# Holding the first weight transfers of a fused RWKV-7 and GELU kernel behind the decays of chunk 1

## The chip, the cores and the metric

The kernel runs on one core of a Trainium2 chip. The metric is device time in microseconds, the median of several executions; one more execution is taken with the hardware profiler, and all views come from it. The engines are named TensorE (PE; PEld is its weight load), VectorE (DVE), ScalarE (ACT), GpSimd (POOL) and SyncE (SP, which only issues transfers). Each runs its own instructions in the order in which the kernel writes them. Transfers are issued from SyncE's queue or from GpSimd's, and run on the core's 16 DMA engines.

## The reference

An attention block with a recurrent state (RWKV-7), then a feed-forward block with an exact GELU:

```python
batch, n_heads, seq, head_dim = (4, 8, 768, 40)      # r, k, v, w, a, b; w between 0.85 and 0.95
n_tokens, d_model, d_ff = (3072, 320, 2048)          # x, w_in, w_out
...
    for t in range(S):
        ...
        y[:, :, t] = np.einsum('bhd,bhde->bhe', rt, state)
        Sa = np.einsum('bhde,bhe->bhd', state, at)
        state_decay = state * wt[:, :, None, :] - np.einsum('bhd,bhe->bhde', Sa, bt)
        state = state_decay + np.einsum('bhd,bhe->bhde', vt, kt)
...
    h = x @ w_in                                     # x: y as (B*S, H*D)
    g = 0.5 * h * (1.0 + erf(h * inv_sqrt2))
    return (g @ w_out).astype(np.float32)
```

The two weight matrices come as 64-bit floats, and the kernel turns them into 32-bit floats itself.

## The kernel before

The sequence is cut into 12 chunks of 64 steps. Within a chunk the recurrence is written as products of small matrices and the inverse of a triangular one; between chunks only the state is carried. All four batches and eight heads of a chunk are worked on together. A chunk's outputs go through the feed-forward block (`ph`, `gelu`, `po` and later a form with seven products) while later chunks are worked on. The order of all work on all five engines is written out by hand, step by step; each engine runs its share in that order.

The steps of the first chunks that matter here:

- `load_w`, `fetch`, `load_a` (line 194 issues the transfers) bring w, b and a of chunks 0 and 1, in this order, from SyncE. The a rows of chunk 1 land in the tile `spare_raw`. Behind them SyncE issues v (`load_VR(0)`), r (`load_r(0)`), k (`fetch(0, 'k')`) and the second part of the first matrix (`first_load(False, 1)`).
- `logs`, `sums_cum` and `exp_cum` give a chunk's decays: a logarithm on ScalarE, sums over the steps as products on TensorE, an exponential on ScalarE (line 526).
- `flip_b`, `copy_b` (the transposes `nT_ps`, line 571, and the copy at line 645) and `turn_a`, `scale_a` (the transposes `aT_ps`, line 571, and the product at line 625) lay out b and a of a chunk.
- `mask_Z`, `turn_Z`, `start_T`, `square`, `turn_square`, `copy_square` and `add_square` invert chunk 0's triangular matrix by repeated squaring. `start_T` is four additions on GpSimd (line 903).
- `first_load(last, part, at, eng)` brings one part of the first matrix, as raw words, in six transfers (lines 431, 433, 434). Part 0 lands in the tile of the second matrix (`w_out_sb`), in columns that are free until that matrix comes; it is issued from GpSimd's queue.
- `U[n]` is the conversion of one tile of raw words, in the steps a, r, m, b, s and g on VectorE, ScalarE and, for some tiles, GpSimd. `U[0].a` (line 371) is the first to read the raw words, parts 0 and 1 of them.

Tiles that take turns in memory have a common tag and a count of buffers (`bufs=2`); a new tile takes the place of the one before last with that tag, and its first writer waits for the last reader of that one. Waits between engines are derived from what each instruction reads and writes: an instruction that writes where another has written waits for it.

The place of the edit in the written order:

```python
    scale_a(0)
    first_load(False, 0, early(0, 4), eng=nc.gpsimd)
    copy_b(0)
    make_N(0)
    mask_N(0)
    exp_cum(1)
    scale_b(1)
```

On GpSimd's own queue the next instructions behind this `first_load` are those of `start_T(0, nc.gpsimd)`, then `scale_k(0)` (line 610) and the elimination steps `substitute(1, ...)` (lines 833 and 835).

Of the kernel before, what the change touches and what calls it, by code (L numbers as in the profile page):

```python
# [21 lines left out]
def kernel(  # L22
# [46 lines left out]
    nc = tc.nc  # L69
# [209 lines left out]
    early_w = SM.rearrange("p e g n c -> p (e g n c)")[:, :G * H * HP]  # L279
    early_k = work.tile([P, G, NP, P], FP32, tag="rT", name="early_k", bufs=2).rearrange("p g n t -> p (g n t)")  # L280
    ahead = {n: t[:, :G * DM].rearrange("p (g h d) -> p g h d", g=G, h=H) for n, t in (("b", early_b), ("k", early_k))}
# [78 lines left out]
    class Unit:  # L360
# [4 lines left out]
        def a(self):  # L365
            w = self.words()
            n = w.shape[1] // 2
            self.lo, self.hi = (w.rearrange("p (n x) -> p n x", x=2)[:, :, x] for x in range(2))
            both = work.tile([P, LW], UINT32, tag="conv", name="conv", bufs=2)
            self.power, self.mant = both[:, :n], both[:, LW // 2:LW // 2 + n]  # L370
            nc.vector.tensor_scalar(self.power, self.hi, 0x7FF00000, None, ALU.bitwise_and)  # L371
# [30 lines left out]
    def first_load(last, part, at=None, eng=nc.sync):  # L402
# [16 lines left out]
        for x in range(2):  # L419
# [6 lines left out]
            else:  # L426
# [5 lines left out]
                if x:  # L432
                    eng.dma_start(out=words[half(x, D), n], in_=src[x, x, part, :, n])
                    eng.dma_start(out=words[x * HP + D:, n], in_=src[1 - x, x, part, :REST, 0])

    def second_load(f, slot, at=late_raw, eng=nc.sync):

        src = moe_w_out.bitcast(UINT32) if wide_out else moe_w_out
        to = w_out_sb[:, f]
        if wide_out:  # L440
            to = second_raw[f] = at[:, slot * DM:(slot + 2) * DM]
        to, rows = (t.rearrange("p (n m) -> p n m", m=P if wide_out else HP) for t in (to, src[f * P:(f + 1) * P]))
        for n in range(2):
            eng.dma_start(out=to[:, n::2], in_=rows[:, n::2])
# [107 lines left out]
    def turn_part(c, blocks):  # L552
        t = turned_in[c]
        if "part" not in t:
            t["part"] = by_batch(side("part", "conv", 2))
# [60 lines left out]
    def scale_a(c):  # L616
        t = turned_in[c]
        wp = t["wp"].rearrange("p (e n) t -> p e n t" if c > NB else "p (n e) t -> p e n t", e=2)[:, :, :, :C]
        if c < NT:
            aT = work.tile([P, 2, G, NP, C], FP32, tag="aT", name="aT", bufs=2)  # L620
# [33 lines left out]
    def turn_k(c):  # L654
        t = turned_in[c]
        if c >= NB:
            kT = t["k_turned"] = by_batch(side("k_turned", "conv", 2))
            turn(kT, c, "k_turned")
            return
        flip_k(c)  # L660
        copy_k(c)
# [40 lines left out]
    def turn_r(c):  # L702
        if c < NT:
            flip_r(c)
            copy_r(c)
            return
        rT = side("rT", "rT", 2)
        turn(rT.rearrange("p q m (e t) -> p (q m e) t", e=2), c, "r")
        turned_in[c]["rT"] = parts(rT)
# [5 lines left out]
    def copy_r(c):  # L715
        rT = side("rT", "rT", 2)
        nc.scalar.copy(rT, turned_in[c].pop("rT_ps"))
        turned_in[c]["rT"] = parts(rT)
# [135 lines left out]
    def turn_inverse(c):  # L854
        W = inverses[c]
        if c < NB:
            to = turned_in[c].pop("Nb") if c > 1 else work.tile([P, BL * BL], FP32, tag="Nb", name="Nb")
            L, T = to[:, :NBL * BL], to[:, NBL * BL:]
        else:
            L = work.tile([P, NBL * BL], FP32, tag="conv", name="L", bufs=2)  # L860
            T = W.rearrange("p s t -> p (s t)")
# [344 lines left out]

    def half_tile(tag, bufs):
        return work.tile([P, NF // 2, P], FP32, tag=tag, name="half", bufs=bufs)

    def seven(c):  # L1210
        t1, t2, t4 = sums_of_w
        t3 = quarter(0, 1)
        os = [work.tile([P, 2, DM // 2], FP32, tag="os", name="os", bufs=2) for g in range(G)]
        c11, c12, c21, c22 = os[0][:, 0], os[0][:, 1], os[1][:, 0], os[1][:, 1]
# [25 lines left out]
        m1, m2 = yield from products_of(0, (block(0, 0), quarter(0, 0)), (block(0, 1), quarter(1, 0)), apart=True)  # L1240
        s1 = half_tile("conv", 2)
        nc.vector.tensor_tensor(s1, block(1, 0), block(1, 1), ALU.add)
        while between:
            new_state(between.pop(), range(1, G))
        if c >= NCH - 2:
            s2 = half_tile("conv", 2)
        else:
# [28 lines left out]
    class Seven:  # L1276

        def __init__(self, c):
            self.c = c
            self.os = [work.tile([P, 2, DM // 2], FP32, tag="os", name="os", bufs=2) for g in range(G)]  # L1280
            self.c11, self.c12, self.c21, self.c22 = (self.os[n // 2][:, n % 2] for n in range(4))
# [14 lines left out]
        def s1(self):  # L1296
            self.one = half_tile("conv", 2)
            nc.vector.tensor_tensor(self.one, block(1, 0), block(1, 1), ALU.add)  # L1298

        def s2(self):  # L1300
            if self.c >= NCH - 2:
                self.two = half_tile("conv", 2)
            else:
# [94 lines left out]
    def put(c, g):  # L1398
        os = work.tile([P, DM], FP32, tag="os", name="os", bufs=2)
        nc.vector.tensor_copy(os, pos[c][:, g])  # L1400
# [178 lines left out]
    copy_r(1)  # L1579
    spare_rT = words("rT", 2)  # L1580
    first_load(True, 1, spare_raw[:, :LW], eng=nc.sync)
# [706 lines left out]
```

## Time and profile before

| | |
|---|---|
| median of 3 runs | 648.96 us (647.38 to 650.41) |
| the profiled execution | 651.05 us, span 649.3 us |
| TensorE busy | 628.7 us, 97% |
| VectorE, ScalarE, GpSimd busy | 452.6, 375.3, 387.0 us |
| mean granted TensorE clock | 0.993 |
| moved by SyncE's queue, by GpSimd's queue | 56.46 MB, 1.70 MB |

The span runs from the first to the last instruction of the profiled execution; its own time holds what lies around the span too. A row of the timeline gives start and length in us, engine, line of the kernel, operation, the tile written and the tiles read, partitions x elements, the count of instructions put together, and in brackets how long the engine had been idle and what ended that. A row of the stretches gives the stretch, its length, the busy time of PE, PEld, DVE, ACT and POOL (with instructions), the granted TensorE clock, the share of the DMA engines and GB/s. A row of a DMA queue gives packets, MB and the time of the packets as a share of 16 engines; the software queue is GpSimd's, the hardware queue SyncE's. The chain of waits is followed back from the last instruction: at each step to what released it.

### The profile page before, as it was taken

What the parts mean: (1) busy time and instruction counts of PE and PEld (TensorE: products, weight loads), DVE (VectorE), ACT (ScalarE), POOL (GpSimd) and SP (SyncE); (2) the same over time, 40 slices, a digit from 0 to 9 for tenths busy, and PEclk for the clock granted to TensorE, in tenths of its full rate; (3) what the DMA queues carried; (4) which work ended last, traced back from release to release, by engine and by line L of the source; (5) the groups of instructions that cost most, each with busy time, mean ns of one, the idle gap of its engine ahead of it and who ended that gap; (6) DMA issues with size and microseconds to landing.
All of it is one profiled execution on the core that took longest, in us unless ns stands there. A gap on an engine that the chain in (4) does not pass through costs nothing.

```text
span 649.3 us, 32674 instructions
## 1 busy us (share of the span) xinstructions
PE 628.7 (97%) x14652; PEld 557.2 (86%) x14652; DVE 452.6 (70%) x604; ACT 375.3 (58%) x716; POOL 387.0 (60%) x806
## 2 busy tenths in 40 slices
PE   7898999999999999999899999999999999999997
PEld 5787888887878899898898998999989989989877
DVE  1684899986568788585895995995987965623312
ACT  5455875554438474746478487587587586373010
POOL 8488488804828828828717858868858768620000
PEclk9998999999999999999899999999999999999999
DMA  9995658447666125447454455464365350210100
GB/s 137 154 158 119 128 129 174 107 96 129 127 107 121 31 51 110 98 94 129 84 109 100 79 113 103 98 123 98 75 128 96 79 100 5 42 24 12 33 2 21
DMA packets 227054, 60.46 MB, mean 93 GB/s; under 512 B 208539, under 2 KB 225211, under 8 KB 226914
## 3 DMA queue, kind: packets, MB, share of 16 engines
q1 hardware_dynamic: 226042, 56.46, 46.5%
q0 software_dynamic: 592, 1.70, 1.3%
q8 instruction: 115, 1.88, 1.3%
q10 hardware_dynamic: 280, 0.21, 0.1%
q14 instruction: 25, 0.20, 0.1%
HBM read 50.46 MB, written 3.93 MB: 84 GB/s over the span
## 4 chain that ended last, share of the span: by engine, by line
PE 66%; POOL 15%; DVE 7%; issue 4%; ACT 3%; SPq 2%; DMA 2%; POOLq 0%; DVEq 0%; ACTq 0%
PE ph L1385 23%; PE po L1288 17%; POOL W L835 7%; POOL tmp L833 6%; PE QY L139 6%; PE po L1395 3%; PE po L1222 2%; PE J L139 2%; SPq L194 2%; DMA spare_raw<-in_a_dram 2%; PE A_ps L139 1%; PE M_ps L139 1%; PE saT_ps L139 1%; PE av L139 1%; PE RV_ps L139 1%
## 5 line engine op out<-in xcount | busy, mean ns | idle before, releaser
L1385 PE MATMUL ph<-xt,w_in_sb 64*64 64x256 f32 (+1 forms) x3360 | 218.3, 377 | 0.4 <-ACT gt L1389 0.2
L1385 PEld LDWEIGHTS ph<-xt,w_in_sb 64*64 64x64 f32 (+1 forms) x3360 | 173.4, 141 | 30.3 <-issue 1.2
L833 POOL TENSOR_TENSOR tmp<-W,Nb 128x126 f32<-128x126 f32 (+22 forms) x310 | 132.5, 427 | 64.3 <-DVE Nb L848 40.9
L835 POOL TENSOR_TENSOR W<-W,tmp 128x126 f32<-128x126 f32 (+22 forms) x310 | 139.6, 450 | 24.3
L1389 ACT ACTIVATE gt<-ph 128x1024 f32<-128x1024 f32 x48 | 49.2, 1026 | 80.1 <-PE ph L1385 76.6
L1288 PE MATMUL po<-w_out_sb,gt 128*128 128x160 f32 x576 | 84.4, 303 | 0.2 <-DVE gt L1323 0.2
L1288 PEld LDWEIGHTS po<-w_out_sb,gt 128*128 128x128 f32 x576 | 79.4, 190 | 1.8 <-issue 0.3
L1190 ACT COPY turned<-within 8x64 f32<-8x64 f32 (+3 forms) x144 | 46.4, 322 | 10.6 <-DVE within L1179 8.6
L786 POOL TENSOR_TENSOR VR<-VR,upper 128x1024 f32<-128x1024 f32 x8 | 19.3, 2414 | 35.0 <-ACT VR L782 32.8
L564 ACT COPY part<-part 32x256 f32<-32x256 f32 (+1 forms) x112 | 36.1, 322 | 1.7
L1395 PE MATMUL po<-w_out_sb,gt 128*128 128x320 f32 x128 | 36.3, 438 | 0.0
L1064 DVE STREAM_TRANSPOSE sa<-saT 128x1024 f32<-128x1024 f32 x9 | 11.2, 1242 | 35.5 <-ACT saT L1051 35.5
L1073 ACT COPY SM<-sa 32x64 f32<-32x64 f32 (+1 forms) x108 | 31.8, 294 | 2.6 <-DVE sa L1064 1.3
L1395 PEld LDWEIGHTS po<-w_out_sb,gt 128*128 128x128 f32 x128 | 23.7, 190 | 9.8 <-issue 0.5
L1311 DVE TENSOR_TENSOR os<-os,po 128x160 f32<-128x160 f32 x63 | 19.6, 314 | 18.0 <-PE po L1288 10.1
L1308 ACT COPY os<-po 128x160 f32<-128x160 f32 x9 | 2.6, 292 | 46.6 <-PE po L1288 46.5
L374 ACT ACTIVATE conv<-conv,rebias 128x320 uint32<-128x320 uint32 (+1 forms) x26 | 15.8, 621 | 20.1 <-DVE conv L371 19.9
L727 DVE TENSOR_TENSOR A<-A_ps,upper 128x1024 f32<-128x1024 f32 x12 | 14.6, 1219 | 14.0 <-PE A_ps L139 14.0
L1288 PE MATMUL po<-extra,half 128*128 128x160 f32 x160 | 23.3, 299 | 0.5 <-DVE half L1298 0.5
L727 DVE TENSOR_TENSOR SM<-M_ps,upper 128x1024 f32<-128x1024 f32 x12 | 14.7, 1223 | 11.9 <-PE M_ps L139 11.7
L1288 PEld LDWEIGHTS po<-extra,half 128*128 128x128 f32 x160 | 22.2, 190 | 0.7 <-issue 0.7
L848 DVE STREAM_TRANSPOSE Nb<-N 128x1024 f32<-128x1024 f32 x10 | 21.6, 2160 | 0.4 <-ACT N L770 0.4
(302 smaller groups left out, 1287.9 us busy)
## 6 DMA issues: line engine op xcount, KB each, us to landing
VR<-in_v_dram SPq DMA_DIRECT2D x24, 160.0 KB
out_dram<-os SPq DMA_DIRECT2D x46, 80.0 KB
b_rows<-in_b_dram SPq DMA_DIRECT2D x22, 160.0 KB
k_rows<-in_k_dram SPq DMA_DIRECT2D x22, 160.0 KB
a_pairs<-in_a_dram SPq DMA_DIRECT2D x18, 144.0 KB
r_pairs<-in_r_dram SPq DMA_DIRECT2D x36, 72.0 KB
v_pairs<-in_v_dram SPq DMA_DIRECT2D x36, 72.0 KB
a_pairs<-in_b_dram SPq DMA_DIRECT2D x16, 144.0 KB
```

Source lines behind the costliest of these rows:

```text
L139: nc.tensor.matmul(o, lhsT, rhs, start=first, stop=True, skip_group_check=True)
L564: nc.scalar.copy(to[at:at + BL, :, x, z * BL:end], tmp[on:on + BL, e, :, q * BL:q * BL + end - z * BL])
L727: nc.vector.tensor_tensor(to, pt, upper.unsqueeze(1).to_broadcast([P, 2 * G * NP, C]), ALU.mult)
L833: eng.tensor_tensor(t, W[:, :rows, j:j + 1].to_broadcast([P, rows, rest]), Nb[:, j:j + 1, j + 1:].to_broadcast([P, rows, rest]), ALU.mult)
L835: eng.tensor_tensor(W[:, :rows, j + 1:], W[:, :rows, j + 1:], t, ALU.add)
L848: nc.vector.transpose(Nb.rearrange("p s t -> p t s"), N[:, :, :BL].rearrange("p n t -> p t n").unsqueeze(2).to_broadcast([P, BL, 2, NBL]))
L1073: copy(SM[to:to + BL, g].rearrange("p q m c -> p (q m) c")[:, :, d * BL:end], t["sa"][at:at + BL, :, to:to + end - d * BL])
L1190: nc.scalar.copy(tn[to:to + deep, :, at:at + wide], within[0][at:at + deep, :, to:to + wide])
L1288: nc.tensor.matmul(self.pt[at][:, n, :DM // 2], l_[:, f], r_[:, f], start=f == 0, stop=f == NF // 2 - 1)
L1385: nc.tensor.matmul(pt[to:end, x, s], w_in_sb[half(x), kt, p * P + to:p * P + end], xt[half(x), kt], start=kt == 0, stop=kt == NK - 1)
L1389: nc.scalar.activation(gt[:, 4 * q:4 * q + 4].rearrange("p (x s) t -> p x s t", x=2), phs.pop((c, q)), ACT.Gelu)
L1395: nc.tensor.matmul(pos[c][:, g], gt[:, f, g * P:(g + 1) * P], w_out_sb[:, f], start=f == 0, stop=f == NF - 1)
```

## The change

A new step `hold(c, at)` copies eight numbers of chunk c's decays, on ScalarE, into the place where a part of the weights is going to land: two columns, 256 apart, in each of the four tiles of words. `first_load(False, 0, ...)` moves behind `hold(1, ...)` in the written order, so that its transfers, which write the same columns, wait for that copy, which waits for the exponential in `exp_cum(1)`. They are still issued from GpSimd's queue. Besides, tiles that shared places in turn by `bufs=2` get a tag for each place (`conv0` and `conv1`, `aT0` and `aT1`, `rT0` and `rT1`, `os0` and `os1`), chosen by the chunk's or the unit's number.

```diff
-    early_k = work.tile([P, G, NP, P], FP32, tag="rT", name="early_k", bufs=2).rearrange("p g n t -> p (g n t)")
+    early_k = work.tile([P, G, NP, P], FP32, tag="rT1", name="early_k").rearrange("p g n t -> p (g n t)")
...
-            both = work.tile([P, LW], UINT32, tag="conv", name="conv", bufs=2)
+            both = work.tile([P, LW], UINT32, tag=f"conv{self.n % 2 if self.n < 16 or self.n > 20 else (self.n + 1) % 2}", name="conv")
...
+    def hold(c, at):
+
+        to = at.rearrange("p (k n) -> p k n", k=NP)[:, :, :LW // 2:2 * P].bitcast(FP32)
+        given = decays[c][0][:, 0, 0, :2 * NP]
+        nc.scalar.copy(to, given.rearrange("p (k n) -> p k n", k=NP))
+
...
+    for n, unit in enumerate(U):
+        unit.n = n
...
-        aT = turned_in[c]["aT"] = work.tile([P, 2, G, NP, C], FP32, tag="aT", name="aT", bufs=2)
+        aT = turned_in[c]["aT"] = work.tile([P, 2, G, NP, C], FP32, tag=f"aT{c % 2}", name="aT")
...
     scale_a(0)
-    first_load(False, 0, early(0, 4), eng=nc.gpsimd)
     copy_b(0)
     make_N(0)
     mask_N(0)
     exp_cum(1)
+    hold(1, early(0, 4))
+    first_load(False, 0, early(0, 4), eng=nc.gpsimd)
     scale_b(1)
     sums_wT(1)
```

More of the change, by code (lines that the diff above doesn't have):

```diff
@@ L554, in turn_part @@
         if "part" not in t:
-            t["part"] = by_batch(side("part", "conv", 2))
+            t["part"] = by_batch(side("part", f"conv{c % 2}", 1))
             nc.vector.transpose(t["part"].rearrange("p n t -> p (n t)"), t["en"].rearrange("p n t -> p (n t)"))
@@ L619, in scale_a @@
         if c < NT:
-            aT = work.tile([P, 2, G, NP, C], FP32, tag="aT", name="aT", bufs=2)
+            aT = work.tile([P, 2, G, NP, C], FP32, tag=f"aT{c % 2}", name="aT")
             given = t.pop("a_ps").rearrange("p g n (e t) -> p e (g n) t", e=2)
@@ L656, in turn_k @@
         if c >= NB:
-            kT = t["k_turned"] = by_batch(side("k_turned", "conv", 2))
+            kT = t["k_turned"] = by_batch(side("k_turned", f"conv{(c + (c > 4)) % 2}", 1))
             turn(kT, c, "k_turned")
@@ L706, in turn_r @@
             return
-        rT = side("rT", "rT", 2)
+        rT = side("rT", f"rT{(c if c < 2 else c + 1) % 2}", 1)
         turn(rT.rearrange("p q m (e t) -> p (q m e) t", e=2), c, "r")
@@ L715, in copy_r @@
     def copy_r(c):
-        rT = side("rT", "rT", 2)
+        rT = side("rT", f"rT{(c if c < 2 else c + 1) % 2}", 1)
         nc.scalar.copy(rT, turned_in[c].pop("rT_ps"))
@@ L859, in turn_inverse @@
         else:
-            L = work.tile([P, NBL * BL], FP32, tag="conv", name="L", bufs=2)
+            L = work.tile([P, NBL * BL], FP32, tag=f"conv{(c + (c > 4)) % 2}", name="L")
             T = W.rearrange("p s t -> p (s t)")
@@ L1205, in weight_sums, with half_tile @@
         nc.vector.tensor_tensor(to, one_, other, ALU.subtract)
-    def half_tile(tag, bufs):
-        return work.tile([P, NF // 2, P], FP32, tag=tag, name="half", bufs=bufs)
+    def half_tile(n):
+        return work.tile([P, NF // 2, P], FP32, tag=f"conv{n % 2}", name="half")
     def seven(c):
@@ L1212, in seven @@
         t3 = quarter(0, 1)
-        os = [work.tile([P, 2, DM // 2], FP32, tag="os", name="os", bufs=2) for g in range(G)]
+        os = [work.tile([P, 2, DM // 2], FP32, tag=f"os{g}", name="os") for g in range(G)]
         c11, c12, c21, c22 = os[0][:, 0], os[0][:, 1], os[1][:, 0], os[1][:, 1]
@@ L1240, in seven @@
         m1, m2 = yield from products_of(0, (block(0, 0), quarter(0, 0)), (block(0, 1), quarter(1, 0)), apart=True)
-        s1 = half_tile("conv", 2)
+        s1 = half_tile(c)
         nc.vector.tensor_tensor(s1, block(1, 0), block(1, 1), ALU.add)
@@ L1245, in seven @@
         if c >= NCH - 2:
-            s2 = half_tile("conv", 2)
+            s2 = half_tile(c + 1)
         else:
@@ L1279, in __init__ @@
             self.c = c
-            self.os = [work.tile([P, 2, DM // 2], FP32, tag="os", name="os", bufs=2) for g in range(G)]
+            self.os = [work.tile([P, 2, DM // 2], FP32, tag=f"os{g}", name="os") for g in range(G)]
             self.c11, self.c12, self.c21, self.c22 = (self.os[n // 2][:, n % 2] for n in range(4))
@@ L1296, in s1 @@
         def s1(self):
-            self.one = half_tile("conv", 2)
+            self.one = half_tile(self.c + 1 if self.c > 3 else 1)
             nc.vector.tensor_tensor(self.one, block(1, 0), block(1, 1), ALU.add)
@@ L1301, in s2 @@
             if self.c >= NCH - 2:
-                self.two = half_tile("conv", 2)
+                self.two = half_tile(self.c)
             else:
@@ L1398, in put @@
     def put(c, g):
-        os = work.tile([P, DM], FP32, tag="os", name="os", bufs=2)
+        os = work.tile([P, DM], FP32, tag=f"os{g}", name="os")
         nc.vector.tensor_copy(os, pos[c][:, g])
@@ L1579 @@
     copy_r(1)
-    spare_rT = words("rT", 2)
+    spare_rT = words("rT0")
     first_load(True, 1, spare_raw[:, :LW], eng=nc.sync)
```

## The prediction

> **What bounds the kernel now.** I read the page first (busy shares, chain of waits), then the chain's early part in order of time, then the timelines of the five engines over the first 60 us, and last the DMA queues in short windows.
>
> ```profile
> PE 628.7 (97%) x14652; PEld 557.2 (86%) x14652; DVE 452.6 (70%) x604; ACT 375.3 (58%) x716; POOL 387.0 (60%) x806
> 80.00:140.00 60.00, 59.88 (x1248) 51.47 (x1248) 56.55 (x96) 37.55 (x54) 42.43 (x80) 1.00 0.59 126
> 11.98 10.58 DMA spare_raw<-in_a_dram
> 22.70 1.06 PE aT_ps L571 x8
> 23.76 2.52 PE sq L139 x64
> ```
>
> The first row says that TensorE (PE) is occupied for 97% of the span; the second, a stretch's length and the busy times of PE, PEld, DVE, ACT and POOL, that from 80 to 140 us it is never free (59.88 of 60 us). PE runs its instructions in the written order, so what delays it in the ragged first 60 us is passed on to the end, as long as the engines that feed it move along. The last three rows are the chain of waits: it runs through one transfer, the rows of a for chunk 1 (they land in the spare tile), for 10.58 us, and then through TensorE's transposes of these rows and the squarings.
>
> ```profile
> 10.81 2.19 SPq L194 DMA_DIRECT2D spare_raw<-in_a_dram  x2
> 11.26 2.70 POOL L431 DMA_DIRECT2D w_out_sb<-in_moe_w_in_dram  x4 [0.25 <-issue]
> 13.92 0.59 POOL L433 DMA_DIRECT2D w_out_sb<-in_moe_w_in_dram  x1
> 14.46 0.57 POOL L434 DMA_DIRECT2D w_out_sb<-in_moe_w_in_dram  x1
> q0 software_dynamic: 368, 1.05, 10.0%
> q0 software_dynamic: 97, 0.30, 84.2%
> q1 hardware_dynamic: 333, 0.05, 25.0%
> 20.23 1.04 PE L571 MATMUL nT_ps<-ident,extra 128*128 128x128 f32 x8
> 22.70 1.06 PE L571 MATMUL aT_ps<-ident,spare_raw 128*128 128x128 f32 x8 [1.43 <-DMA spare_raw<-in_a_dram]
> ```
>
> These are timeline rows (start, length) and, between them, DMA queues (packets, MB, share): GpSimd's over the first 60 us, where its 1.05 MB are the six weight transfers, and then GpSimd's and SyncE's from 18 to 20 us. While SyncE issues the a rows, GpSimd (POOL) issues the six weight transfers that the change holds. In the narrow window GpSimd's queue moves 0.30 MB and SyncE's 0.05 MB: the a rows crawl behind weights that nobody reads until 35.66 us (below). TensorE ends the transposes before them at 20.23 + 1.04 = 21.27, and stands 1.43 us for the a rows.
>
> **The change, part by part.** The naming of tiles by place: put side by side engine by engine, the two built programs hold the same instructions in the same order; every tile keeps the partners it shared a place with and only whole places lie at other addresses. I see no row by which that costs or gains, so 0. What is left is one ScalarE copy more, six DMA issues on GpSimd moved behind it, and two waits that follow from it (GpSimd's first held transfer, and SyncE's first transfer of the second weight part, both on that copy).
>
> *The copy.* It stands on ScalarE behind the exponential that gives the decays of chunk 1.
>
> ```profile
> 2.11 0.20 ACT L298 ACTIVATE one<-one 128x1 f32<-128x1 f32 x1
> 16.84 0.70 ACT L526 ACTIVATE avs<-cum 128x640 f32<-128x640 f32 x1
> 19.13 1.03 ACT L515 ACTIVATE wpT<-wT_ps 128x1024 f32<-128x1024 f32 x1 [1.59 <-PE wT_ps L139]
> ```
>
> The decays end at 17.54; the smallest ScalarE operation here is 0.20 us, so the copy ends about 17.9 with the hand-over. ScalarE then idles until 19.13 (1.59 us): cost 0. Without that cover it would be 0.3.
>
> *What is removed.* The a rows meet no weights. Their nearest undisturbed relative is w of chunk 1, of the same size:
>
> ```profile
> 6.22 2.01 SPq L194 DMA_DIRECT2D SM<-in_w_dram  x2
> 12.60 1.28 ACT L476 ACT_TABLE_LOAD   x1 [1.00 <-DMA SM<-in_w_dram]
> ```
>
> From the end of its issue (8.23) to its landing, about 12.60, are 4.4 us. The a rows' issue ends at 13.00, so they land near 17.4, 3.9 us ahead of 21.27. The whole 1.43 us goes; more cannot, since the transposes ahead on TensorE do not move (their inputs were on their way before 11.26 us).
>
> *What is late next.* GpSimd's instructions queue behind the held transfers, first among them start_T (L903), whose result the first squaring with T needs.
>
> ```profile
> 20.50 5.25 POOL L903 TENSOR_TENSOR SM<-SM,ident 32x512 f32<-32x512 f32 x4 [5.47 <-ACT wpT L515]
> 27.19 1.07 ACT L922 COPY SM<-sq 128x512 f32<-128x512 f32 x2 [4.82 <-DVE Nb L919]
> 28.36 1.54 PE L139 MATMUL sq<-SM,Nb 64*64 64x96 f32 x32 [1.09 <-issue]
> ```
>
> The six issues take 2.70 + 0.59 + 0.57 = 3.86 us (rows above). From 17.9 they end at 21.7, so start_T runs from about 21.8 to 27.0 and not to 25.75. That squaring now waits for ScalarE's copy (27.19 + 1.07 = 28.26); 1.43 earlier this is 26.83. GpSimd's 27.0 then comes last by about 0.15 us. Net gain there: 1.43 - 0.15 = 1.3 us.
>
> The issues' own price on GpSimd has two ends. With VectorE (DVE) nearly idle, as before, one is 3.86 / 6 = 0.64; beside a busy VectorE the nearest row is this:
>
> ```profile
> 85.63 1.58 POOL L444 DMA_DIRECT2D w_out_sb<-in_moe_w_out_dram  x2
> 18.32 0.81 DVE L602 SCALAR_TENSOR_TENSOR extra<-early_b,avs 128x640 f32<-128x640 f32 x1
> 20.39 1.25 DVE L899 STREAM_TRANSPOSE Nb<-SM 128x1024 f32<-128x1024 f32 x1
> ```
>
> that is 0.79 each, 4.7 for six, start_T's end at 27.9 and a gain of 0.4 us. I take the lower price, since most of VectorE's work between 17.9 and 21.7 is one long operation at a time out of PSUM or a transpose; beside that transpose start_T's pieces kept their 1.26 us. The Trainium skill, "SBUF — State Buffer", section "SBUF: two separate sides", speaks against this move: GpSimd cannot write the descriptors of its transfers while VectorE holds the port pair that both share, and a transfer of about 620 ns then took about 3100. By that figure a single issue caught would end start_T near 29.5, and turn the gain into a loss of about 1.2 us (an estimate from that page). The row at 85.63, beside operations of VectorE, shows 0.79 and no such stop.
>
> *The other transfers.* SyncE's queue behind the a rows is v, r, k and the second weight part.
>
> ```profile
> 13.04 4.92 SPq L254 DMA_DIRECT2D VR<-in_v_dram  x2
> 18.00 6.82 SPq L267 DMA_DIRECT2D r_pairs<-in_r_dram  x4
> 24.87 1.36 SPq L194 DMA_DIRECT2D k_rows<-in_k_dram  x2
> 47.64 2.01 SPq L254 DMA_DIRECT2D VR<-in_v_dram  x2
> 83.09 3.05 SPq L267 DMA_DIRECT2D r_pairs<-in_r_dram  x4
> 29.83 1.09 PE L571 MATMUL rT_ps<-ident,r_pairs 128*128 128x128 f32 x8
> 30.21 1.55 POOL L610 TENSOR_TENSOR extra<-k_rows,part 128x640 f32<-128x640 f32 x1 [4.47 <-DMA k_rows<-in_k_dram]
> 35.66 0.47 DVE L371 TENSOR_SCALAR conv<-w_out_sb 128x512 uint32<-128x512 uint32 x1
> ```
>
> Issues of v and r took 4.92 and 6.82 us beside the weights, and take 2.01 and 3.05 elsewhere. So v is issued by 15.1, r by 18.1, k by 19.5, each over 5 us earlier than before. From about 19 the held weights share the engines with the rest of r and k. Even at 0.05 MB in 2 us for SyncE's queue through the 7 us that 1.05 MB of weights need at 0.30 MB in 2 us, r (wanted at 28.4) and k (wanted by GpSimd at 27.0, where it idled 4.47 us for k anyway) are no later than before, because everything ahead of them left earlier. U[0].a at 35.66 is the first reader of the weights, of both parts, and VectorE runs in order behind it.
>
> ```profile
> 22.00:24.00 2.00, 1.30 (x18) 1.17 (x20) 0.10 (x1) 0.37 (x1) 1.93 (x2) 1.00 0.93 108
> 24.00:26.00 2.00, 2.00 (x60) 1.81 (x55) 1.74 (x2) 0.00 (x0) 1.69 (x2) 1.00 0.66 103
> 32.00:34.00 2.00, 2.00 (x42) 1.76 (x40) 1.65 (x2) 0.78 (x2) 0.67 (x3) 1.00 1.13 211
> ```
>
> The last column is GB/s. Before, the engines ran at 103 to 108 in the middle of this work, after the weights, and were done with the second part shortly ahead of 35.66. With a queue that is never empty I expect no slack of that kind and a landing near 32 to 33, ahead of the 34.4 at which U[0].a now comes: cost 0.
>
> *The sum.* The profiled execution takes 651.05 us for a span of 649.3, 1.75 lying around the span. 651.05 - 1.3 = 649.75. It is 2.09 over the median of the runs shown (648.96), so on the median's scale 648.96 - 1.3 = **647.7 us**, 0.2% faster. Faster or slower by 0.5% (3.2 us) is about what a measurement of this kernel can tell from no change, and the runs shown span 647.38 to 650.41.
>
> **The rivals.** *No gain left.* GpSimd's issues beside VectorE, or a feeder further on (the conversions of the weights on VectorE and GpSimd around 80 us), eat the 1.3 us: 648.6 to 649.0, and up to 650.2 if one issue is caught for 2.5 us behind an operation of VectorE, which no row here shows. For it: the long issue row at 85.63. Against: the chain of waits enters the conversions from TensorE's own products, so they move along. That the hold doesn't hold isn't this case: the copy's columns lie under the first held transfer, and the others queue behind it.
>
> *More than the chain shows.*
>
> ```profile
> 52.84 1.51 PE L139 MATMUL J<-SM,W 32*32 32x32 f32 x61 [1.04 <-issue]
> 54.00:56.00 2.00, 2.00 (x20) 1.65 (x15) 0.69 (x1) 1.61 (x3) 1.61 (x6) 0.50 0.23 55
> 55.29 1.75 PE L571 MATMUL kT_ps<-ident,extra 128*128 128x128 f32 x8
> 62.72 1.04 PE L571 MATMUL rT_ps<-ident,v_pairs 128*128 128x128 f32 x8
> ```
>
> Between 54 and 56 us TensorE's granted clock is 0.50, and eight transposes take 1.75 where they take 1.04: at least 0.7 us lost there, about 1.2 with the filler products beside them. TensorE also stands 1.04 us at 51.8 for nothing that the profile shows. If transfers that come earlier take both away, the gain is 1.43 + 1.2 + 1.04 = 3.7: 645.3 us. The Trainium skill, "TensorE: Matmul & The Clock Gate", Part 1, has the clock halved after a window of about 3.4 us with little work, windows that run free of the kernel's start; the trace agrees with the half clock. By that rule the slow stretch can as well come back elsewhere, which is why this stays a rival.
>
> *Slower: the weights come too late.* Place: U[0].a. The 1.05 MB of the second part follow r and k in SyncE's queue, and these now share the engines with the held part. If the engines then move the second part at the 103 GB/s of 24 to 26 us and not at the 211 of 32 to 34, it takes 10 us from about 28 (19 + 7 for the held part, and what is left of r and k), lands at 38.5 to 39.5, and VectorE, with all squarings behind it, stands till then: 3 to 4 us over the 35.66 of before, 652.5 us. It decides from a landing after 35.7. For it: before, the second part's last packets were only about a microsecond ahead of its reader. Against: the low rate came with queues that SyncE filled late.
>
> **How the numbers follow.** Forecast 0.46, no gain left 0.18, more than the chain 0.24, weights too late 0.12. Faster by over 0.5% is the third (645.3 is 3.7 under): 0.24; within it the first two: 0.64; slower 0.12. The range takes in the first three with about 1 us of the runs' spread below 645.3, and above 649.0 the spread of the slow end and of half a late landing: 644.3 to 651.4; the late landing's own 652.5 stays outside.
>
> **What would show it.** Right: the six issues begin near 17.9 on GpSimd; the a rows' transposes follow their predecessors at 21.3 with no wait for a DMA; start_T ends near 27.0 and the first squaring with T starts there; U[0].a comes near 34.4 without a wait on a DMA; and all later stages lie 1.3 us earlier. Wrong: issues on GpSimd over 0.8 us each, a wait of VectorE at U[0].a, or an end that moves by more than the first 35 us did.

## The result, and the profile after

The changed kernel takes 654.61 us (median of 20 runs, 651.98 to 660.49), the kernel before on the same chip 650.85 us (20 runs, 647.38 to 655.69). The ratio, which goes by the means and not by the medians, is 1.0068, with an interval of 1.0046 to 1.0091: slower by 0.7%, where 0.2% faster was forecast, and outside the range. The profiled execution took 657.39 us for a span of 655.7, at a mean granted clock of 0.982 (before 0.993). A second profile of the changed kernel, taken later (called "again" below), took 658.29 us. Executions that lie more than 1.5% above the fastest of their kernel are left out of all ratios and clocks below: one of twelve of act_queue, start_T_first, filled_hole, before_filled and J_filled each, and three of the 99 of the kernel before.

The changed kernel's timelines of ScalarE, GpSimd and TensorE around the edit (start, length, engine, line, operation; in brackets the idle time ahead and what ended it; line numbers behind line 440 are 6 to 8 higher than before):

```profile
16.68 0.71 ACT L534 ACTIVATE avs<-cum 128x640 f32<-128x640 f32 x1
17.41 0.21 ACT L440 COPY w_out_sb<-avs 128x8 f32<-128x8 f32 x1
17.93 2.69 POOL L431 DMA_DIRECT2D w_out_sb<-in_moe_w_in_dram  x4 [7.21 <-ACT w_out_sb L440]
20.60 0.56 POOL L433 DMA_DIRECT2D w_out_sb<-in_moe_w_in_dram  x1
21.14 0.53 POOL L434 DMA_DIRECT2D w_out_sb<-in_moe_w_in_dram  x1
21.68 5.29 POOL L911 TENSOR_TENSOR SM<-SM,ident 32x512 f32<-32x512 f32 x4
27.00 1.07 ACT L930 COPY SM<-sq 128x512 f32<-128x512 f32 x2 [4.85 <-POOL SM L911]
20.94 1.04 PE L579 MATMUL aT_ps<-ident,spare_raw 128*128 128x128 f32 x8
24.39 1.10 PE L139 MATMUL N_ps<-aT,nT 40*64 40x64 f32 x62
28.18 2.56 PE L139 MATMUL sq<-SM,Nb 64*64 64x96 f32 x32 [2.69 <-issue]
30.66 1.68 PE L579 MATMUL rT_ps<-ident,r_pairs 128*128 128x128 f32 x8
```

Down to start_T all is as forecast: the copy hides, the issues begin at 17.93 and take 3.78 us, the transposes of the a rows no longer wait, start_T ends at 26.97. Then the row of L930: ScalarE's copy of the square waits for start_T (`<-POOL SM L911`). It writes Z, which start_T is still reading. So copy and squaring come one after the other behind start_T, TensorE stands 2.69 us, and the squaring starts at 28.18 at half speed: 2.56 us where 1.54 were taken, the transposes behind it 1.68 where 1.09.

The kernel before gave a surprise too. The rows below are TensorE's squaring, J (the first corner product of chunk 0's inverse) and X (the first product of the state with chunk 1's a) in a second profile of it (650.88 us); then J and X in its first profile, in the changed kernel, and in the changed kernel again:

```profile
26.91 1.54 PE L139 MATMUL sq<-SM,Nb 64*64 64x96 f32 x32 [1.33 <-issue]
45.79 1.50 PE L139 MATMUL J<-Nb,N 32*32 32x32 f32 x64 [0.87 <-DVE Nb L930]
72.05 1.14 PE L139 MATMUL X<-st,aT 40*64 40x40 f32 x64
```

```profile
47.26 1.39 PE L139 MATMUL J<-Nb,N 32*32 32x32 f32 x64 [0.87 <-DVE Nb L930]
72.65 1.14 PE L139 MATMUL X<-st,aT 40*64 40x40 f32 x64
```

```profile
48.73 0.31 PE L139 MATMUL J<-Nb,N 32*32 32x32 f32 x8 [0.89 <-DVE Nb L938]
80.66 1.14 PE L139 MATMUL X<-st,aT 40*64 40x40 f32 x64
```

```profile
48.63 1.88 PE L139 MATMUL J<-Nb,N 32*32 32x32 f32 x64 [0.86 <-DVE Nb L938]
79.52 1.14 PE L139 MATMUL X<-st,aT 40*64 40x40 f32 x64
```

In the second profile of before the squaring starts at 26.91, not 28.36: the a rows were there in time without any hold. So against such an execution the change makes the squaring 1.3 us later, not earlier. The half clock there adds to it, J begins 2.8 to 2.9 us late against that second profile, and from J to X the changed kernel takes 31.9 and 30.9 us instead of 25.4 and 26.3. The stretches of TensorE show why (stretch, length, busy time with instructions, granted clock, DMA share, GB/s), in before's second profile, the changed kernel, and the changed kernel again:

```profile
28.00:32.00 4.00, 4.00 (x70) 1.00 1.02 203
48.00:56.00 8.00, 7.44 (x223) 0.85 0.64 126
56.00:64.00 8.00, 6.22 (x246) 1.00 0.79 167
```

```profile
28.00:32.00 4.00, 3.82 (x39) 0.57 1.14 200
48.00:56.00 8.00, 6.99 (x160) 0.56 0.55 121
56.00:64.00 8.00, 8.00 (x206) 0.59 0.69 156
```

```profile
28.00:32.00 4.00, 3.52 (x37) 0.57 1.13 207
48.00:56.00 8.00, 7.37 (x179) 0.55 0.61 130
56.00:64.00 8.00, 6.83 (x220) 0.81 0.72 153
```

The changed kernel runs at about half clock between 28 and 32 and again for 10 to 14 us of the 16 from 48 to 64 (twice what the clock lacks to 1, times the stretch); in the kernel before it is 3.5 us and, from 48 on, 2.4 (in that second profile it begins ahead of 48, at a clock of 0.73 from 46 to 48). Two more terms lie on the way to X. The last part of TensorE's product M_ps, in before's second profile, in the changed kernel, and in the changed kernel again:

```profile
59.47 0.39 PE L139 MATMUL M_ps<-rT,saT 40*64 40x64 f32 x10 [0.73 <-issue]
```

```profile
67.65 0.58 PE L139 MATMUL M_ps<-rT,saT 40*64 40x64 f32 x10 [2.92 <-issue]
```

```profile
65.71 0.54 PE L139 MATMUL M_ps<-rT,saT 40*64 40x64 f32 x10 [2.54 <-issue]
```

The changed kernel stands about 2 us longer in the middle of this product, for nothing that the profile shows, and behind it comes a third stretch at half clock: 0.57 and 0.59 from 66 to 74 us, where before's second profile has 1.00. The moved transfers alone don't make that stop: in J_filled, below, they are as late, and it is 0.74 us and in a second profile 0.47.

Both profiled executions of the changed kernel lie in the slower half of its runs; the loss in the median is smaller than their 8 us at X.

The clock of every run fits this without a profile. In 96 runs of the kernel before that were made beside the experiments the mean granted clock is 0.9933, and a line through them gives 5.7 us for each 0.01 of clock. The changed kernel's 20 runs have 0.9862, which by that line is 4.0 us. Measured: 4.4 us between the means, 3.8 between the medians. Such a line shows that time and clock go together, not which of them sets the other; the runs with filled holes, below, test that.

### The profile page after: what moved, and what is told of

Same layout as the page of the kernel before. It is cut to its first block, busy times and chain, and to the rows that moved or that the text cites. A ratio compares the mean times of both kernels' runs of the same rounds, so it can differ in the third digit from the quotient of the medians.

```text
span 655.7 us, 32675 instructions
## 1 busy us (share of the span) xinstructions
PE 634.3 (97%) x14652; PEld 560.9 (86%) x14652; DVE 451.5 (69%) x604; ACT 376.0 (57%) x717; POOL 390.1 (59%) x806
## 4 chain that ended last, share of the span: by engine, by line
PE 63%; POOL 16%; DVE 8%; issue 4%; ACT 4%; SPq 3%; DMA 1%; DVEq 0%; POOLq 0%; ACTq 0%
PE ph L1393 21%; PE po L1296 17%; POOL W L843 6%; POOL tmp L841 6%; PE QY L139 5%; PE po L1403 3%; PE po L1230 2%; PE J L139 2%; PE av L139 2%; PE saT_ps L139 2%; PE A_ps L139 1%; PE M_ps L139 1%; PE X L139 1%; PE RV_ps L139 1%; SPq L194 1%
## 5 line engine op out<-in xcount | busy, mean ns | idle before, releaser
L1393 PEld LDWEIGHTS ph<-xt,w_in_sb 64*64 64x64 f32 (+1 forms) x3360 | 172.3, 141 | 31.9 <-issue 1.3
L841 POOL TENSOR_TENSOR tmp<-W,Nb 128x126 f32<-128x126 f32 (+22 forms) x310 | 131.0, 423 | 64.5 <-DVE Nb L856 41.1
L843 POOL TENSOR_TENSOR W<-W,tmp 128x126 f32<-128x126 f32 (+22 forms) x310 | 143.9, 464 | 24.3
L1081 ACT COPY SM<-sa 32x64 f32<-32x64 f32 (+1 forms) x108 | 31.9, 295 | 2.6 <-DVE sa L1072 1.3
```

The lines of the kernel that those rows point to most:

```text
L841: eng.tensor_tensor(t, W[:, :rows, j:j + 1].to_broadcast([P, rows, rest]), Nb[:, j:j + 1, j + 1:].to_broadcast([P, rows, rest]), ALU.mult)
L843: eng.tensor_tensor(W[:, :rows, j + 1:], W[:, :rows, j + 1:], t, ALU.add)
L1081: copy(SM[to:to + BL, g].rearrange("p q m c -> p (q m) c")[:, :, d * BL:end], t["sa"][at:at + BL, :, to:to + end - d * BL])
L1393: nc.tensor.matmul(pt[to:end, x, s], w_in_sb[half(x), kt, p * P + to:p * P + end], xt[half(x), kt], start=kt == 0, stop=kt == NK - 1)
```

## The experiments

The theories: (1) the late start_T makes the hole at 25.5 to 28.2, and hole and clock make the loss; (2) the weight transfers, now 6.7 us later, crowd the later transfers and TensorE's instructions; (3) the new places of the tiles cost something. All ratios are against the kernel before on the same chip, 11 or 12 runs each (20 of the changed kernel); the clock is the mean over the same runs.

| kernel | ratio | interval | clock |
|---|---|---|---|
| changed kernel | 1.0068 | 1.0046 to 1.0091 | 0.986 |
| names_only | 0.9983 | 0.9947 to 1.0020 | 0.994 |
| act_queue | 1.0044 | 1.0004 to 1.0084 | 0.992 |
| start_T_first | 1.0033 | 0.9993 to 1.0074 | 0.992 |
| delay_T | 1.0020 | 0.9985 to 1.0055 | 0.990 |
| hold_sooner | 0.9994 | 0.9956 to 1.0033 | 0.992 |
| filled_hole | 1.0018 | 0.9975 to 1.0061 | 0.991 |
| J_filled | 1.0050 | 1.0021 to 1.0080 | 0.993 |
| filled_two | 0.9972 | 0.9941 to 1.0002 | 0.998 |
| before_filled | 0.9982 | 0.9948 to 1.0016 | 0.995 |
| before_J_filled | 1.0027 | 0.9999 to 1.0055 | 0.993 |
| sooner_J_filled | 0.9996 | 0.9964 to 1.0027 | 0.995 |

**names_only: only the naming by place.** The transfers go back to their old place, without the hold:

```diff
     scale_a(0)
+    first_load(False, 0, early(0, 4), eng=nc.gpsimd)
     copy_b(0)
...
-    hold(1, early(0, 4))
-    first_load(False, 0, early(0, 4), eng=nc.gpsimd)
```

> The changed kernel without its copy and with the six transfers issued from GpSimd where they were before: only the naming of the places is left. Theory 1 (the held issues delay start_T on GpSimd, TensorE then stands from 25.5 to 28.2 us, and its clock is halved after that): ratio to the kernel before 1.000, within 0.003. Theory 2 (the moved transfers crowd the DMA engines later on, where data and TensorE's instructions come late, whatever start_T does): 1.000 too. Theory 3 (the shifted addresses cost the time): 1.005 to 1.009, as the changed kernel.

0.9983: theory 3 is out. Its profile has the a rows in time once more (aT_ps at 21.34 with no wait). ScalarE's copy of the square waits for start_T there too:

```profile
26.04 1.07 ACT L930 COPY SM<-sq 128x512 f32<-128x512 f32 x2 [3.43 <-POOL SM L911]
```

Of the six profiles taken in this order of transfers (before, before again, names_only, delay_T, before_filled, before_J_filled) two show the wait, with 1.43 and 0.82 us; a mean of 0.4.

**act_queue: the six transfers on ScalarE's queue**, behind `copy_b(1)`, without the hold:

```diff
-    hold(1, early(0, 4))
-    first_load(False, 0, early(0, 4), eng=nc.gpsimd)
...
     copy_b(1)
+    first_load(False, 0, early(0, 4), eng=nc.scalar)
```

> No copy and no transfer on GpSimd: the six transfers are issued from ScalarE's queue behind copy_b(1), from about 22 to 26 us, where ScalarE idles, so that GpSimd runs start_T at 20.4 as before. The a rows still meet no weights. Theory 1: start_T ends at 25.7, the first squaring with T begins near 26.9, clock 1.00 from 28 to 32, ratio 0.996 to 0.999. Theory 2: the weights share the engines with what follows as in the changed kernel or worse, 1.005 or more, with TensorE's long stop near 64 us. Theory 3: 1.005 to 1.009.

ScalarE's part of the timeline, and the squaring:

```profile
21.53 2.77 ACTq L431 DMA_DIRECT2D w_out_sb<-in_moe_w_in_dram  x4
24.34 0.77 ACTq L433 DMA_DIRECT2D w_out_sb<-in_moe_w_in_dram  x1
26.94 0.31 ACTq L434 DMA_DIRECT2D w_out_sb<-in_moe_w_in_dram  x1
27.34 1.07 ACT L930 COPY SM<-sq 128x512 f32<-128x512 f32 x2 [4.82 <-DMA w_out_sb<-in_moe_w_in_dram]
28.52 1.81 PE L139 MATMUL sq<-SM,Nb 64*64 64x96 f32 x32 [2.72 <-issue]
```

start_T was on time (20.65 to 25.94), but now ScalarE's own issues, with a pause of 1.8 us in them, hold up the same copy: the same hole of 2.7 us, the clock at 0.70 between 28 and 32, and 1.0044. It doesn't tell 1 from 2, since the hole is there from another cause.

**start_T_first: the hold kept, the six transfers issued behind start_T:**

```diff
     hold(1, early(0, 4))
-    first_load(False, 0, early(0, 4), eng=nc.gpsimd)
...
     start_T(0, nc.gpsimd)
+    first_load(False, 0, early(0, 4), eng=nc.gpsimd)
```

> As the changed kernel, but the six transfers are issued from GpSimd behind start_T, from about 25.8 to 29.6 us. Theory 1: the first squaring with T begins near 26.9, no half clock from 28 to 32; 0.997 to 1.000, or up to 1.003 if U[0].a, wanted near 34.4, now waits for the first part, which would land at 34 to 36. Theory 2: the weights come later still and the crowding moves later: 1.007 or more. Theory 3: 1.005 to 1.009.

The squaring starts at 27.11 with full clock to 36 us. The weights, issued from 25.85 to 29.60, bring a new stop further on (VectorE, then TensorE):

```profile
37.23 0.63 DVE L371 TENSOR_SCALAR conv<-w_out_sb 128x512 uint32<-128x512 uint32 x1 [2.81 <-issue]
38.85 0.80 PE L139 MATMUL A_ps<-aT,kT 40*64 40x64 f32 x19 [2.65 <-issue]
```

The first names the reader of the weights; the second stands in the middle of a product whose inputs were there, so the weights' landing is not all of it. J comes at 49.56, X at 73.91, and the ratio is 1.0033. Its interval takes in 1 as well as the changed kernel's 1.0068, so what weights that come too late cost is not shown.

**delay_T: start_T late, no transfer moved.** This is names_only with one more addition ahead of start_T's four:

```diff
     def start_T(c, eng):
+        rows, cols = quads[0]
+        eng.tensor_tensor(sq["T"][rows, :12], sq["Z"][rows, :12, cols], ident[rows, rows].unsqueeze(1).to_broadcast([BL, 12, BL]),
+                          ALU.add)
```

> The kernel before (with the tiles named by place, which cost nothing) and one more GpSimd addition of 32x384 ahead of start_T, about 0.97 us by the 1.32 us of its 32x512 additions. No transfer is moved and there is no copy into the weights' place. start_T should begin near 20.7 and end near 27.0, as in the changed kernel. Theory 1 (the loss comes from the late start_T: ScalarE's copy of the square waits for it, TensorE stands still for 2.7 us and falls to half clock): the first squaring with T begins near 28.2, half clock shows between 28 and 32, and the time is slower than before by 0.3 to 0.7% (2 to 4.5 us). Theory 2 (the loss comes from the weight transfers that run 6 us later and crowd the later transfers and TensorE's instructions): the first squaring is late too, but the time is that of before within 0.3%.

1.0020, inconclusive: both theories' numbers lie in the interval. The added operation took 0.99 us, start_T ran from 21.52 to 26.76, and the copy waited 4.48 us for it. In the profile the a rows were late by 0.82 us, so the hole was only 1.36 us, and the clock stayed full at 28 to 32. The half clock behind J was longer than before's (0.67 between 48 and 56), and the mean clock, 0.990, is low. That lateness alone suffices is not shown.

**hold_sooner: the copy behind the logarithms of chunk 1**, out of them, 2.7 us sooner:

```diff
     logs(1)
+    hold(1, early(0, 4))
+    first_load(False, 0, early(0, 4), eng=nc.gpsimd)
...
-    hold(1, early(0, 4))
-    first_load(False, 0, early(0, 4), eng=nc.gpsimd)
...
-        given = decays[c][0][:, 0, 0, :2 * NP]
+        given = raws[c, "w"][:, :2 * NP]
```

> The changed kernel with the 8 columns copied right behind the logarithms of chunk 1 (out of them) in place of behind its decays: about 2.9 us sooner. GpSimd's six issues then run near 15.1 to 18.9 and start_T begins on time near 20.7; the a rows still land ahead of the transfers. Theory 1: the first squaring with T begins near 27.2, no half clock between 28 and 32, and the time is that of before or a little less (-0.3 to +0.1%). Theory 2: the transfers are still 4 us later than before, so most of the loss stays: slower by 0.3 to 0.7%, with TensorE standing still on its own instructions for 2 to 3 us somewhere between 60 and 70.

0.9994, median 651.18: theory 1's number. start_T begins at 20.50, the squaring at 26.98. The a rows are in time, and the loss is gone, though the weights' issue begins at 15.22, 4 us later than before (6.7 in the changed kernel). That speaks against theory 2; filled_two, below, leaves the transfers as late as the change made them and has no loss either. The profile fell on one of its two executions of twelve over 658, with half clock all through 48 to 56. A second profile was taken:

> A second profile of the kernel with the sooner copy; the first fell on one of its two executions of twelve near 658.5. In an ordinary one (650 to 651.5) the first squaring begins near 27.0, and behind the hole ahead of J there is at most one stretch of 3 to 4 us at half clock. If the stretch of 48 to 57 at half clock is there again, the sooner copy doesn't spare it and theory 1 is wrong on what the late start_T does to J.

The stretch behind J in the first profile of hold_sooner, and in the second:

```profile
48.00:56.00 8.00, 8.00 (x156) 0.50 0.65 116
```

```profile
48.00:56.00 8.00, 7.25 (x228) 0.79 0.69 119
```

With one short stretch at half clock X comes at 71.06, earlier than in the kernel before; with a long one at 79.11. So start_T on time doesn't always spare J the long stretch. The second execution took 656.86 us all the same, from a later stop that comes below.

**filled_hole, filled_two and J_filled: TensorE kept busy in its holes**, by products that nobody reads, in the changed kernel: ahead of the squaring (`filled_hole`, 1280 columns), ahead of that and of J (`filled_two`, 768 columns there), or ahead of J alone (`J_filled`, `keep(2)`, 256 columns):

```diff
+    keep(4, 4, 2)
     square(1, 0)
...
+    keep(4, 2)
     corner_direct(0)
```

> The changed kernel with filler products (10 x 128 columns, about 2.2 us, into a place that is written over) on TensorE ahead of the first squaring with T, in the stop from 25.5 to 28.2 us. Theory 1 in its clock part: the granted clock stays at 1.00 from 28 to 32, the second squaring comes near 30.7 and not at 32.3, ratio 1.002 to 1.005, better than the changed kernel by 1.5 us or more. If only the late start_T mattered and not the clock, or by theory 2 or 3: as the changed kernel, 1.007.

> The changed kernel with TensorE kept busy (matmuls whose product nobody reads) in two of its holes: ahead of the first squaring with T (1280 columns, as tried before) and ahead of the first corner product J near 48 (768 columns). If the second half clock, 49 to 62.7 in the changed kernel's trace, starts from the hole ahead of J, it is gone here and with the first fill the time is that of before within 0.2%. If it has another cause, 0.50 to 0.60 shows again between 49 and 62 and the time stays near the 0.2 to 0.4% that the first fill alone left.

> The changed kernel with only the hole ahead of the first corner product J filled: 256 columns of unread matmuls, 0.70 us of the 0.88. The hole of 2.7 us ahead of the first squaring with T stays. Theory 1a (what costs time is the half clock that begins at J and lasts up to 14 us; how long depends on where J falls, which the change moved by 1.4 to 2.6 us): mean granted clock over the runs above 0.992, and slower than before by no more than 0.3%. Theory 1b (the first hole costs by itself, by the half clock between 28 and 32): half clock still shows there, mean clock near 0.989, slower by 0.4 to 0.7%.

Two stretches of filled_hole, of filled_two and of J_filled:

```profile
28.00:32.00 4.00, 3.38 (x57) 1.00 1.14 207
48.00:56.00 8.00, 7.47 (x176) 0.53 0.66 138
```

```profile
28.00:32.00 4.00, 3.37 (x57) 1.00 1.13 202
48.00:56.00 8.00, 7.43 (x209) 1.00 0.61 116
```

```profile
28.00:32.00 4.00, 3.50 (x36) 0.58 1.13 204
48.00:56.00 8.00, 6.83 (x208) 1.00 0.63 131
```

Each fill takes away the half clock at its own hole and leaves the other. X begins at 79.77, 73.91 and 74.17. With both filled the clock is 0.998, no run is under 0.994, and the ratio is 0.9972 where the changed kernel had 1.0068, though start_T is as late as ever and the added products do nothing. That shows that holes and clock carry the loss. Filling the first hole takes the ratio from 1.0068 to 1.0018, and from 1.0050 to 0.9972 where J is filled; filling J takes it from 1.0068 to 1.0050, and from 1.0018 to 0.9972, though at X it brings 3 to 7 us. By these figures the first hole counts more, but only the step from 1.0050 to 0.9972 is clear of its intervals, so which of the two counts more is not shown. J_filled met neither theory's numbers whole: the clock of 1a (0.993), the time and the half clock between 28 and 32 of 1b. Two second profiles were to tell why:

> A second profile of the changed kernel with only the hole ahead of J filled. If what it wins ahead of X (74.17 against 80.66) is given back by the collision of VectorE and GpSimd behind it, chunk 2's elimination waits for VectorE's Nb again, TensorE waits for ScalarE's nT, and po follows po in 28 us or more. If the first profile was an accident, it follows in 26.7 and the run ends near 651.

> A second profile of the changed kernel with only the first hole filled. By theory 1 the clock is full between 28 and 32 again; behind J half clock may or may not show, since the mean clock over its twelve runs (0.991) lies between that of the changed kernel (0.986) and that with both holes filled (0.998).

J_filled again took 650.32 us, with X at 73.88; the first time it was 657.94 with X at 74.17. So its X is no accident, and the difference lies behind X. VectorE, GpSimd and TensorE there in the first profile, and then in the second:

```profile
91.09 1.27 POOL L395 TENSOR_TENSOR w_in_sb<-conv 128x512 f32<-128x512 f32 x1
91.45 1.60 DVE L618 TENSOR_TENSOR extra<-k_rows,avs 128x640 f32<-128x640 f32 x1
92.32 1.88 POOL L394 TENSOR_TENSOR conv<-conv,gt 128x512 f32<-128x512 f32 x1
96.97 1.09 POOL L841 TENSOR_TENSOR tmp<-W,Nb 128x31 f32<-128x31 f32 x1 [0.79 <-DVE Nb L856]
137.71 1.92 PE L139 MATMUL N_ps<-aT,nT 40*64 40x64 f32 x64 [0.98 <-ACT nT L653]
```

```profile
89.78 0.84 DVE L618 TENSOR_TENSOR extra<-k_rows,avs 128x640 f32<-128x640 f32 x1
90.00 1.75 POOL L395 TENSOR_TENSOR w_in_sb<-conv 128x512 f32<-128x512 f32 x1
94.78 0.42 POOL L841 TENSOR_TENSOR tmp<-W,Nb 128x31 f32<-128x31 f32 x1
135.31 1.11 PE L139 MATMUL N_ps<-aT,nT 40*64 40x64 f32 x64
```

VectorE's scaling of k meets the same GpSimd addition (line 395) in both, and it matters which begins first. In the second profile the scaling does, and takes 0.84 us while the addition takes 1.75; in the first the addition began 0.36 us ahead, takes 1.27, and the scaling takes 1.60. GpSimd's elimination for chunk 2 then starts late, its result comes late 30 us on, ScalarE's copies queue behind that, and TensorE stands for nT and falls to half clock again: 30.7 us from one product `po` to the next, where it is 26.2. Of eighteen profiles the two of hold_sooner and four of the six with a filled J show this wait for nT, with 28 to 31 us between these products; the others don't (26.2 to 27.1). In those six, and in no other, the addition begins first. Why VectorE comes later there is not settled. hole_again has full clock at 28 to 32 and 0.68 from 48 to 64, X at 77.23, as theory 1 said; its 660.29 us come from stops further on that were not followed up.

**before_filled, before_J_filled and sooner_J_filled: the fills without the loss.** The first is names_only with 768 columns ahead of both holes, the second names_only with `keep(2)` ahead of J, the third hold_sooner with the same:

```diff
+    keep(2)
     corner_direct(0)
```

> The kernel before (tiles named by place) with the same two holes of TensorE filled, by 768 columns each. If holes that let the clock fall are worth time in the kernel before as well, it is faster than before by 0.2 to 0.5%; if the clock falls only where the change made a longer hole, the time is that of before within 0.2%, and the fills cost at most the 0.3 us by which they could run past the holes' ends.

> The kernel before (tiles named by place) with the same 256 columns ahead of J. If the half clock at J costs the kernel before 2 to 4 us in some of its executions too, the mean clock rises from 0.993 to 0.996 or more and the time falls by 0.2 to 0.4%. What it then lacks against the run with the sooner copy is what the hold itself is worth: by the waits for the a rows in four profiles of this order (1.43, 0, 0.82 and 0 us) about 0.1%.

> The changed kernel with the 8 columns copied behind the logarithms of chunk 1, so that start_T is on time, and the hole ahead of J filled by 256 columns. If both causes are named rightly, nothing is late and the clock does not fall: mean granted clock 0.995 or more, no run below 0.987, and faster than before by 0.2 to 0.5% (649 to 651.5). If the late weight transfers cost time by themselves, it is no faster than before.

0.9982, 1.0027 and 0.9996: no gain, against what I expected of the last two. The clock does what was said in the third (0.995, no run below 0.989) and not in the second (0.993); in the first it is 0.995 too. The time doesn't follow, perhaps in part by the collision just shown, which is in the profiles of the second and the third. Set beside each other, before_filled (0.9982) and filled_two (0.9972) have both holes filled, on the same chip, and differ in the change (and in the length of the first fill): what is left of the change without its holes, the squaring at 28.37 and not at 27.03 included, costs nothing that these runs can tell. No version beats both kernels beyond its interval.

**The kernels themselves again:**

> A second profile of the changed kernel, to tell what recurs. By theory 1 the copy of the square waits for start_T again (end near 27.0), the first squaring begins near 28.2 after a hole of 2.7 us, and half clock shows behind it or behind the hole ahead of J; stops of TensorE at its own instructions may fall elsewhere. The a rows are there in time again.

> A second profile of the kernel before. If the wait for the a rows is an accident of single executions, it may be 0 to 1.4 us here; the hole ahead of J (0.87) should be there again, with half clock behind it or not, and the second product of the experts (po) 26.7 us behind the first.

Both as expected: the changed kernel repeats hole, copy and half clocks (rows above), and the kernel before has no wait for the a rows, and half clock once behind J.

## Why the prediction was wrong

- **Naming, copy, issues: right.** 0.9983 for the naming alone. The copy took 0.21 us in ScalarE's idle time, the issues 3.78 us for the 3.86 forecast. None was caught behind VectorE for the 3.1 us of the page "SBUF — State Buffer" of the Trainium skill, section "SBUF: two separate sides": the largest group of four took 2.69.
- **The wait that goes: right in the mechanism, wrong in the size.** The a rows never wait behind the hold. But the term of 1.43 us was read from one execution, and the wait was there in two of six, 0.4 us in the mean. That left less to win than the 1.3 us of the sum from the start.
- **start_T's end at 27.0: right. What waits for it: wrong, and this is the step that failed.** I took the squaring for the only reader and let ScalarE's copy end at 26.83 beside it. The copy overwrites Z, which start_T reads, so it begins only when start_T has ended. Copy (1.07) and hand-over come on top, and the squaring starts at 28.18. The row of before that I quoted named VectorE as the releaser of that copy, since there the a rows had made VectorE last; the other condition, GpSimd, was met 1.4 us sooner and so not shown. In names_only and in hold_sooner, where the a rows are in time, the same row names GpSimd. Against executions in which the a rows are in time (squaring at 26.91 and 27.21) the step loses 1.0 to 1.3 us, where a gain of 1.3 was booked.
- **The clock: only priced as a gain.** The prediction held that the half clock "can as well come back elsewhere", gave that no price, and used the clock gate for a rival on the fast side alone. The hole of 2.7 us brought it back at once, and behind J it lasted 10 to 14 us. This, and not the 1.0 to 1.3 us by themselves, is what the runs show as the loss (filled_two beside before_filled). The Trainium skill, "TensorE: Matmul & The Clock Gate", Part 1, has the clock fall after an idle window of about 3.4 us and rise after a busy one. The fall fits, in that filling the holes prevents it, though the hole ahead of J is only 0.87 us long. The rise doesn't: between 48 and 56 us in hold_sooner TensorE shows 8.00 of 8 us busy at a clock of 0.50. What does fit is the length: the half clock behind J comes in steps of about 3.4 us (last section).
- **The rival on the slow side had the wrong place.** U[0].a came at 36.69 without a wait for a DMA; it followed the late squarings. The weights were in time, and with start_T on time their later transfer cost nothing that could be measured (hold_sooner).

Open is how much of the loss each hole makes by itself, what decides how long the half clock behind J lasts (not J's lateness alone: act_queue has J at 48.77 and about 3.4 us of it, hold_sooner has J at 46.01 and about 10), and whether the late start_T would make the whole loss without the moved transfers.

## What to carry to other kernels

Before you delay a step, list all that must wait for its end: the readers of its result, and also the writers of what it reads; the profile names only the releaser that came last, and the next one may be a microsecond behind it. A wait of about a microsecond seen in one profile should be seen in a second before it is booked as a gain. And where TensorE is nearly always busy, a hole of 2 to 3 us can cost more than its length: price it with a stretch at half clock behind it.

## What the runs showed of the hardware

- A hole of 0.86 to 0.89 us ahead of J was followed by half clock in all eleven profiles that have it, though in two (before's first and hold_sooner's second) only about 6 us after J began, behind further holes of 0.55 to 1.04 us. A hole of such a length is not enough by itself: behind one of 0.86 us at 53 in J_filled (0.84 in its second profile) and one of 0.67 ahead of J in start_T_first the clock stayed full up to 62.
- The half clock behind J came in steps of about 3.4 us. From 46 to 66 us the mean clock is 0.91 in five of the eleven profiles, 0.83 in one, 0.74 in three and 0.65 to 0.66 in two; twice what is lacking, times 20 us, is 3.6, 6.8, 10.4 and about 14 us.
- TensorE stops inside a run of like products, for nothing that the profile shows, at the same places of its program and for different times: behind the 54th product of M_ps 0.25 us in the kernel before, 0.73 in its second profile, and 2.92 and 2.54 in the changed kernel. In the changed kernel SyncE's queue has 112% of the 16 engines' time in the six microseconds from 60 on.
- In one profile (act_queue) transfers issued from ScalarE's queue held up ScalarE's next copy by a pause of 1.8 us between issues, where GpSimd's six issues took 3.8 us without one.
- Where a VectorE product of 128x640 and a GpSimd addition of 128x512 meet, the one that begins later takes longer: in the twelve profiles in which VectorE begins first it takes 0.81 to 0.89 us and the addition 1.74 to 1.92; in the six others the addition takes 1.27 and VectorE 1.58 to 1.87.
